# Factors turned by VectorE, a lighter start, and other queues for three pairs' loads, in a state-space and bilinear kernel

## Chip, core and metric

One core of a Trainium2 chip. The metric is the device time of one execution in microseconds, lower is better; the number used is the median over several runs.

## The reference

Two layers, one after the other. The first is a chunked state-space scan over 4 batches, 8 heads, 768 tokens, head width 32, state width 16; the second is a bilinear feed-forward over all 3072 tokens.

```
log_a = log(clip(a, 1e-06, 1))
for each chunk c of 32 tokens:                      # per batch and head
    cum = cumsum(log_a[chunk])
    M = (C B^T) * exp(cum_i - cum_j) * causal
    y[chunk] = M x + (C state) * exp(cum_i)
    state = exp(sum log_a) * state + sum_j B_j x_j exp(cum_last - cum_j)
x2 = y as [3072, 256]                               # token by (head, width)
out = (x2 @ w_a * (x2 @ w_b)) @ w_out               # d_ff = 1536
```

## The kernel before

The kernel uses chunks of 128 tokens instead of 32, six blocks of them, and puts two of the four batches into a *pair*: pair p is block p // 2, batches 2 (p % 2) and the next. There are 12 pairs. Instead of a table of decays it scales B and C. `scan` (VectorE) forms the running products Pr of a in each block; `over_mid` takes the reciprocal rmid of the product at the block's middle. The factors fC = Pr times rmid, by token on partitions, and fB = 1 / fC are made in `factors_mm`: small matmuls of Pr with a selection table selr (which `sel_over_mid` scales by rmid) turn Pr from head-on-partition to token-on-partition. Line 260 is the form for pairs 0 to 3, line 248 that for blocks 2 to 5. The result bank fps is copied to fC by ScalarE (`factors`).

For each pair `scale_bc` multiplies B by fB (bm) and C by fC (cm, or planes for later pairs). The matrices are then turned, by TensorE and copies for pairs 0 to 3 (`transposes`), by a DMA transpose on SP's queue for the others (`turn`, tile `turned`). `scores` multiplies them into the score banks SC, `mask` applies the causal mask (three quarters on VectorE, one on GpSimd behind a ScalarE copy `tmp`), `scale_x` makes x in float16, and `pv` or `outputs` forms y, in X2T or XB, and the state sums. `state_sums` and `state_spread` carry the state from block to block.

The feed-forward runs in units between these steps: `unit` multiplies a pair's y by a slice of Wa and of Wb (tiles aps, bps), ScalarE copies aps to asb (`evac_a`), VectorE multiplies (`times`, hk); `bunit` is the same for a whole block. `out_half` and `bout` multiply hk by Wo and store. All matmul results outside the scores go to four PSUM banks in the order of the string `BANKS`, one digit for each.

The order of the work is written out by hand and kept by each engine. Each engine's own queue also issues its loads: in `load1` one half of a pair (128 KB of x, 64 KB of B or C), in `load2` both halves in one DMA. `loads_bc(p)` issues C and B of pair p, by default from SP's queue, `loads_x(p)` x. Pairs share three input buffers, so a pair's load waits for the readers of the pair three before. SP's queue also carries the turnings and the stores, in order. The weights Wa, Wb, Wo are loaded by GpSimd's queue in two halves each, Wa's first half behind the mask tables (ident at line 201, causal at line 205), which GpSimd fills, and three loads of pair 1 (line 148).

```python
    def loads_bc(p):
        if p < NP:
            tiles(p)
            for w in (1, 0):
                load2(nc.sync, p, w)
```

Of the kernel before, what the change touches and what calls it, by code (L numbers as in the profile page):

```python
# [10 lines left out]
f32 = mybir.dt.float32  # L11
f16 = mybir.dt.float16
# [7 lines left out]
YS = 16.0  # L20

BANKS = (
    "0123102310231012301230123012031230123013201320130213021302130213021320312031203102132013"
    "2013203102310231023103210321032103210321032103210231023102310231023102310231023102310231"
)


# [1 line left out]
def kernel(  # L29
# [66 lines left out]
    planes = [big.tile([128, 6, H * N], f16, name=f"planes{t}") for t in range(2)]  # L96
    causal_q = big.tile([128, Q], f16, name="causal_q")
    Pr = big.tile([BH, NBLK, Q], f32, name="Pr")
    rmid = big.tile([BH, NBLK], f32, name="rmid")
    selr = big.tile([BH, NBLK, 2, NBP * H], f32, name="selr")  # L100
    fB = big.tile([128, NBLK, 2, NBP, H], f32, name="fB")
# [25 lines left out]
    def bank(name):  # L127
        return psf.tile([128, 512], f32, name=name, tag=f"ff{next(banks)}")
# [58 lines left out]
    load1(nc.sync, 1, 0, 0)  # L187
    nc.sync.dma_start(c32, p32_t.ap())
    nc.vector.memset(warm.bitcast(u32), 0)
    nc.vector.memset(zero, 0.0)  # L190
    nc.gpsimd.memset(sel, 1.0)
    nc.gpsimd.affine_select(
# [5 lines left out]
        pattern=[[-H, 2], [-2 * H, NBP], [-1, H]],  # L198
        channel_multiplier=1,
    )  # L200
    nc.gpsimd.memset(ident, 1.0)
    nc.gpsimd.affine_select(
        out=ident, in_=ident, compare_op=ALU.is_equal, fill=0.0, base=0, pattern=[[-1, 128]], channel_multiplier=1
    )
    nc.gpsimd.memset(causal, 1.0)
    for bt in range(2):
        v = causal[64 * bt : 64 * bt + 64]
        nc.gpsimd.affine_select(  # L208
# [16 lines left out]
    def scan(lo, hi):  # L225
        for k in range(lo, hi):
            nc.vector.tensor_tensor_scan(Pr[:, k], a_sb[:, k], zero, 1.0, ALU.mult, ALU.add)
# [12 lines left out]
    def factors_mm(lo, hi, fps=None, k0=0):  # L240
        if fps is None:
            fps = bank("fps")
        w = 2 * NBP * H
        F = fps[:, k0 * w : (k0 + hi - lo) * w].rearrange("p (k r c) -> p k r c", k=hi - lo, r=2)
        for k in range(lo, hi):
            if k * NBP >= P0:
                for c0 in (0, 64):
                    nc.tensor.matmul(
                        F[c0 : c0 + 64, k - lo].rearrange("p r c -> p (r c)"),
                        Pr[:, k, c0 : c0 + 64],  # L250
                        selr[:, k].rearrange("p t c -> p (t c)"),
                        start=True,
                        stop=True,
                        skip_group_check=True,
                        tile_position=(0, c0),
                    )
                continue
            for r in range(2):
                for bt in range(2):
                    nc.tensor.matmul(  # L260
                        F[64 * bt : 64 * bt + 64, k - lo, r],
                        Pr[:, k].rearrange("p (i r) -> p r i", r=2)[:, r],
                        selr[:, k, bt],
                        start=True,
                        stop=True,
                        skip_group_check=True,
                        tile_position=(0, 64 * bt),
                    )
        return F.rearrange("p k r c -> p (k r c)")

    def factors(lo, hi, fps):
        factors_mm(lo, hi, fps)
        nc.scalar.copy(flat(fC, lo, hi), fps[:, 0 : (hi - lo) * 2 * NBP * H])

    def flat(f, lo, hi):
        return f[:, lo:hi].rearrange("p k r b h -> p (k r b h)")

# [4 lines left out]
    def scale_x(p, eng):  # L282
# [5 lines left out]
        else:  # L288
            eng.tensor_scalar(xo, xi, XS, None, ALU.mult)  # L289

    def scale_bc(p, which, eng, factor=None):
        blk, bp = divmod(p, NBP)
        name, f = (("bm", fB), ("cm", fC))[which]
        raw = by_token(pair_in[p][which]) if p >= P0 else pair_in[p][which].rearrange("p h r n -> p r h n")
        if p >= P0 and which:
            eng.tensor_tensor(  # L296
                out=planes[p % 2][:, 4:6].rearrange("p t (h n) -> p t h n", n=N),
                in0=raw,
                in1=f[:, blk, :, bp].unsqueeze(3).broadcast_to((128, 2, H, N)),
                op=ALU.mult,  # L300
            )
            return
        m_ = mid.tile([128, 2, H, N], f16, name=name, tag=name)
        eng.tensor_tensor(  # L304
            out=m_,
            in0=raw,
            in1=(f[:, blk, :, bp] if factor is None else factor).unsqueeze(3).broadcast_to((128, 2, H, N)),
            op=ALU.mult,
        )
        st.setdefault(p, {})[name] = m_  # L310
        if p >= P0:
            dst = planes[p % 2][:, 0:4].rearrange("p (t e) (m f n) -> p t e m f n", e=2, f=2, n=N)
            for e in range(2):
                eng.tensor_copy(dst[:, :, e, :, e], m_.rearrange("p t (m f) n -> p t m f n", f=2)[:, :, :, e])

    def transposes(p, ps=None, between=None, apart=False):
        s = st[p]
        if ps is None:
            ps = [SC[0], SC[1]] if apart else None
            on_dve = apart  # L320
        else:
            on_dve = True
        TB, TC = (TT[:, 0:256], TT[:, 256:512]) if ps is None else [t_.bitcast(f16)[:, 0:256] for t_ in ps]
        for T_, src in ((TB, s["bm"]), (TC, s["cm"])):
            for r in range(2):
                nc.tensor.transpose(
                    T_[:, r * 128 : (r + 1) * 128], src[:, r].rearrange("p h n -> p (h n)"), ident
                )
            if between:
                between()  # L330
                between = None
        BT = mid.tile([128, 2, 2, 2, 64], f16, name="bt", tag="bt")
        CT = mid.tile([128, 2, Q], f16, name="ct", tag="ct")
        b_ = []
        for e in range(2):
            o_ = BT[:, e].rearrange("p r t i -> p (r t i)")
            b_.append(nc.scalar.activation(out=o_, in_=TB, func=AF.Copy, scale=par[:, e : e + 1]))
        c_ = (nc.vector.tensor_copy if on_dve else nc.scalar.copy)(
            CT.rearrange("p t (i r) -> p r (t i)", r=2), TC.rearrange("p (r c) -> p r c", r=2)
        )  # L340
        if apart:
            for i_ in b_:
                tc.declare_no_dep(c_.ins, i_.ins.name, reason="reads of two banks")
        s["BT"], s["CT"] = BT, CT

# [250 lines left out]
    def unit_mm(p, k2, W):  # L596
# [13 lines left out]
                )  # L610
        return ps

    def evac_a(a_ps, on_dve=False):
        asb = ffh.tile([128, 512], f32, name="asb", tag="asb")
        (nc.vector.tensor_copy if on_dve else nc.scalar.copy)(asb, a_ps)  # L615
        return asb
# [90 lines left out]
            eng = nc.gpsimd if (blk, c) == (NBLK - 2, 3) else (nc.sync, nc.scalar)[part]  # L707
            eng.dma_start(rows[:, cs], o_sb[:, 0:w])  # L708

    def loads_bc(p):  # L710
        if p < NP:
            tiles(p)
            for w in (1, 0):
                load2(nc.sync, p, w)

    def loads_x(p, eng=None):
        if p < NP:
            load2(eng or nc.gpsimd, p, 2)

    def fb(k):  # L720
        nc.vector.reciprocal(flat(fB, k, k + 1), flat(fC, k, k + 1))
# [18 lines left out]
    warmup(1, SC[3], 128)  # L740
    scale_bc(0, 0, nc.vector)
    scale_bc(0, 1, nc.vector, v.rearrange("p (r b h) -> p r b h", r=2, b=NBP)[:, :, 0])
    tb, tcp = bank("tb"), bank("tc")
    transposes(0, [tb, tcp], lambda: warmup(1, SC[3], 128))
    nc.scalar.copy(flat(fC, 0, 1), v)
    scan(3, 4)
    warmup(1, SC[3])
    warmup(2, SC[3], 128)
    scores(0)
# [14 lines left out]
    pv_u(0, 1, py, True)  # L764
    for bt in range(2):
        evac0(1, bt, (nc.scalar, nc.vector)[bt], py)
    scan(4, 5)
    w1 = load_w(1)
    for bt in range(2):
        load1(nc.gpsimd, 2, 0, bt)  # L770
    warmup(1, tcp, 128)
    transposes(1, apart=True)
    scan(5, NBLK)
    over_mid(1, NBLK)
    sel_over_mid(1, NBLK, nc.vector)
    aps = [unit_mm(0, 0, Wa), unit_mm(0, 1, Wa)]
    asb = [evac_a(aps[0])]
    nc.gpsimd.tensor_tensor(out=hr, in0=Pr[:, 0:NG, Q - 1], in1=rmid[:, 0:NG], op=ALU.mult)
    nc.gpsimd.tensor_tensor(out=hs, in0=hr, in1=Pr[:, 1:NBLK, 63], op=ALU.mult)
    nc.gpsimd.tensor_tensor(  # L780
# [2 lines left out]
        in1=selb.rearrange("p (b g) -> p b g", b=nb),  # L783
        op=ALU.mult,
    )
    scores(1)
    mask(product(1, 3), by_pool=True)
    aps.append(unit_mm(0, 2, Wa))
    asb.append(evac_a(aps[1]))
    asb.append(evac_a(aps[2]))  # L790
    fps = bank("fps")
    factors(1, NBLK, fps)
    scale_x(1, nc.scalar)
    for m in range(3):
        mask(product(1, m))
    bps = [unit_mm(0, k2, Wb) for k2 in range(3)]
    for bt in range(2):
        load1(nc.gpsimd, 2, 1, bt)
    load_wo(0)
# [9 lines left out]
    for c0 in (0, 64):  # L809
# [7 lines left out]
            tile_position=(0, c0),  # L817
        )
    nc.scalar.copy(G.rearrange("p b g -> p (b g)"), gps[:, 0 : nb * NG])
    for k2 in range(1, 3):  # L820
        times(0, k2, bps[k2], asb[k2])
    fb(1)
# [26 lines left out]
    h = unit(1, 5)  # L849
    scores(2)  # L850
    mask(product(2, 3), by_pool=True)
    mask(product(2, 0))
    mask(product(2, 1))
    mask(product(2, 2))
    h()
    scale_x(2, nc.scalar)
    scale_bc(3, 0, nc.gpsimd)
    scale_bc(3, 1, nc.gpsimd)
    loads_bc(5)
    o = [bank("ops"), bank("ops")]  # L860
    out_mm(0, 0, o[0], range(6))
    out_mm(0, 1, o[1], range(6))
# [59 lines left out]
        return [lambda k=k: bunit(blk, k) for k in ks]  # L922

    scores(3)
    prep(4, (2,))
    mask(product(3, 3), by_pool=True)
    loads_bc(6)
    prep(5)
    loads_x(4, nc.sync)
    loads_x(5, nc.sync)  # L930
# [125 lines left out]
```

## Time and profile before

| | |
|---|---|
| runs | 122.92, 123.72, 124.85; median 123.72 us |
| profiled execution | 122.51 us, span 120.8 us, granted TensorE clock 0.999 |
| busy, share of the span | TensorE 96%, VectorE 71%, ScalarE 60%, GpSimd 52% |
| first unit (line 601) starts | 10.58 us |
| DMA moved | 13.73 MB in 66641 packets, 61616 of them under 512 bytes |
| loads of B or C, 128 KB by SP's queue | median 4.1 (C) and 4.6 us (B) from issue to landing |
| turnings | eight, median 3.2 us from issue to landing |

The span is the time between the first and the last event of the core; the measured time lies 1.7 us above it. An engine's busy share says how much it ran, not that it set the end. In a timeline row the columns are start, duration, engine, line and operation, output and input, and in brackets how long the engine stood idle before it and what released it. `PE` is TensorE, `DVE` VectorE, `ACT` ScalarE, `POOL` GpSimd, `SPq` SP's queue.

### The profile page before, as it was taken

Reading aid. Unit: us, or ns where it says so; the run is one execution under the profiler, and the core shown is the slowest. Engines: PE = TensorE matmul, PEld = TensorE weight load, DVE = VectorE, ACT = ScalarE, POOL = GpSimd, SP = SyncE. Lnnn points to the kernel's source line nnn. Section 1 sums busy time; section 2 is a strip of 40 time slices with the busy share of each in tenths; the row PEclk is TensorE's granted clock in tenths of the full one; section 3 lists DMA queues with packets and bytes.
Section 4 is the critical chain, followed back from the end, with each engine's and each line's share of the span. In section 5 each row is a group of like instructions: output and inputs, shape, how many; then the busy total and the mean of one; then the engine's idle time right before and its main releaser. Section 6 shows DMA issues by size and latency. Waiting matters only on the chain.

```text
span 120.8 us, 3711 instructions
## 1 busy us (share of the span) xinstructions
PE 115.7 (96%) x1455; PEld 79.4 (66%) x1455; DVE 85.2 (71%) x162; ACT 72.1 (60%) x142; POOL 62.3 (52%) x108
## 2 busy tenths in 40 slices
PE   5889999999999999999999999999999999999990
PEld 2445889888898898644476464766464684555890
DVE  1887888882989898499984999677799445847100
ACT  0466757854965767877668637645646737566220
POOL 7999998972795676299731993138400000000200
PEclk9999999999999999999999999999999999999999
DMA  3999999986969999699998874869501012010032
GB/s 62 171 169 233 173 201 159 215 140 70 100 99 126 128 125 144 111 135 146 71 151 111 173 239 126 91 90 159 180 3 49 0 43 87 0 49 0 20 110 87
DMA packets 66641, 13.73 MB, mean 114 GB/s; under 512 B 61616, under 2 KB 66256, under 8 KB 66624
## 3 DMA queue, kind: packets, MB, share of 16 engines
q1 hardware_dynamic: 62448, 9.40, 50.7%
q0 software_dynamic: 2176, 3.74, 17.0%
q10 hardware_dynamic: 2000, 0.36, 1.6%
q8 instruction: 11, 0.18, 0.7%
q14 instruction: 6, 0.05, 0.1%
HBM read 11.13 MB, written 3.15 MB: 118 GB/s over the span
## 4 chain that ended last, share of the span: by engine, by line
PE 89%; DMA 4%; POOL 3%; issue 0%; ACT 0%; POOLq 0%
PE ops L694 18%; PE aps L667 18%; PE bps L667 17%; PE ops L637 9%; PE aps L601 9%; PE bps L601 9%; DMA Wa<-in_moe_w_a_dram 4%; PE SC L358 2%; PE SC L419 2%; POOL cn L148 1%; PE SC L373 1%; PE SC L433 1%; PE SC L508 1%; POOL bn L148 1%; POOL causal L208 1%; PE SC L460 1%
## 5 line engine op out<-in xcount | busy, mean ns | idle before, releaser
L615 ACT COPY asb<-aps 128x512 f32<-128x512 f32 x72 | 41.8, 586 | 14.1 <-PE aps L667 9.7
L679 DVE TENSOR_TENSOR hkb<-bps,asb 128x512 f16<-128x512 f32 x48 | 32.3, 687 | 12.8 <-ACT asb L615 11.6
L667 PE MATMUL aps<-XB,Wa 128*128 128x512 f16 x96 | 28.6, 379 | 0.0
L667 PE MATMUL bps<-XB,Wb 128*128 128x512 f16 x96 | 28.5, 379 | 0.0
L694 PE MATMUL ops<-Wo,hkb 128*128 128x256 f16 (+1 forms) x204 | 22.5, 267 | 0.0
L694 PEld LDWEIGHTS <-hkb 128*128 128x128 f16 x204 | 18.5, 98 | 3.1
L413 DVE TENSOR_TENSOR t<-SC,causal_q 128x512 f16<-128x512 f32 x27 | 17.1, 681 | 3.3 <-PE SC L358 3.3
L622 DVE TENSOR_TENSOR hk<-bps,asb 128x512 f16<-128x512 f32 x24 | 16.2, 685 | 2.4 <-ACT asb L615 1.2
L667 PEld LDWEIGHTS <-Wb 128*128 128x128 f16 x96 | 9.9, 103 | 10.9
L667 PEld LDWEIGHTS <-Wa 128*128 128x128 f16 x96 | 9.7, 103 | 9.1 <-issue 0.2
L708 POOL DMA_DIRECT2D out_dram<-osb x1 | 0.6, 639 | 27.3 <-ACT osb L706 27.3
L706 ACT ACTIVATE osb<-ops 128x256 f32<-128x256 f32 (+1 forms) x16 | 6.0, 376 | 14.3 <-PE ops L694 14.2
L601 PE MATMUL aps<-X2T,Wa 128*128 128x256 f16 x96 | 14.0, 273 | 0.1
L601 PE MATMUL bps<-X2T,Wb 128*128 128x256 f16 x96 | 13.8, 273 | 0.0
L637 PE MATMUL ops<-Wo,hk 128*128 128x256 f16 x96 | 11.5, 273 | 0.0
L601 PEld LDWEIGHTS <-Wa 128*128 128x128 f16 x96 | 9.5, 104 | 1.1 <-DMA Wa<-in_moe_w_a_dram 0.3
L601 PEld LDWEIGHTS <-Wb 128*128 128x128 f16 x96 | 9.8, 103 | 0.6
L411 POOL TENSOR_TENSOR t<-tmp,causal_q 128x512 f16<-128x512 f32 x5 | 5.8, 1159 | 8.0 <-ACT tmp L410 7.9
L637 PEld LDWEIGHTS <-hk 128*128 128x128 f16 x96 | 8.9, 98 | 1.4
L304 POOL TENSOR_TENSOR bm<-bn,fB 128x256 f16<-128x256 f32 x11 | 7.1, 641 | 4.8 <-DMA bn<-in_B_dram 3.6
L289 POOL TENSOR_SCALAR x<-xn 128x512 f16<-128x512 f32 x6 | 8.9, 1489 | 1.0 <-DMA xn<-in_x_dram 0.7
L296 POOL TENSOR_TENSOR planes<-cn,fC 128x256 f16<-128x256 f32 x8 | 5.0, 621 | 7.9 <-DMA cn<-in_C_dram 7.8
(95 smaller groups left out, 124.0 us busy)
## 6 DMA issues: line engine op xcount, KB each, us to landing
out_dram<-osb SPq DMA_DIRECT2D x22, 128.0 KB, 1.8
xn<-in_x_dram SPq DMA_DIRECT2D x7, 256.0 KB, 4.3
cn<-in_C_dram SPq DMA_DIRECT2D x8, 128.0 KB, 4.1
bn<-in_B_dram SPq DMA_DIRECT2D x8, 128.0 KB, 4.6
Wa<-in_moe_w_a_dram POOLq DMA_DIRECT2D x2, 384.0 KB, 5.9
Wb<-in_moe_w_b_dram POOLq DMA_DIRECT2D x2, 384.0 KB, 7.3
Wo<-in_moe_w_out_dram POOLq DMA_DIRECT2D x2, 384.0 KB, 7.2
xn<-in_x_dram POOLq DMA_DIRECT2D x4, 128.0 KB, 7.2
```

What stands on the lines that cost most here:

```text
L289: eng.tensor_scalar(xo, xi, XS, None, ALU.mult)
L304: eng.tensor_tensor(out=m_, in0=raw, in1=(f[:, blk, :, bp] if factor is None else factor).unsqueeze(3).broadcast_to((128, 2, H, N)), op=AL ...
L411: nc.gpsimd.tensor_tensor(out=o_, in0=tmp, in1=c_, op=ALU.mult)
L413: nc.vector.tensor_tensor(out=o_, in0=i_, in1=c_, op=ALU.mult)
L601: nc.tensor.matmul(ps[:, kk * 2 * Q : (kk + 1) * 2 * Q], W[k // 6][:, f, k % 6 // 3 * 384 : (k % 6 // 3 + 1) * 384].rearrange("p (c kk) -> ...
L615: (nc.vector.tensor_copy if on_dve else nc.scalar.copy)(asb, a_ps)
L622: nc.vector.tensor_tensor(out=s["hk"][:, 2 * k2 : 2 * k2 + 2, :].rearrange("p k q -> p (k q)"), in0=b_ps, in1=asb, op=ALU.mult)
L637: nc.tensor.matmul(o_ps[:, 0:d_model], hk[:, k, bt * Q : (bt + 1) * Q], Wo[:, k, :], start=(k == 0), stop=(k == NK - 1), skip_group_check= ...
L667: nc.tensor.matmul(t_, W[k // 6][:, f, k % 6 // 3 * 384 : (k % 6 // 3 + 1) * 384].rearrange("p (c kk) -> p kk c", kk=3)[:, k % 3], XB[:, b ...
L679: return lambda: nc.vector.tensor_tensor(out=s["hk"][:, k], in0=ps[1], in1=asb, op=ALU.mult)
L694: nc.tensor.matmul(o_ps[:, 0:w], hk[:, k, c * Q : (c + 1) * Q], Wo[:, k, cs], start=(k == 0), stop=(k == NK - 1), skip_group_check=True,)
L706: nc.scalar.activation(out=o_sb[:, 0:w], in_=o_ps[:, 0:w], func=AF.Copy, scale=1.0 / (YS * YS))
```

## The change

- The memsets of `ident` and `causal` go from GpSimd to VectorE, after its first memset; GpSimd keeps the selects on them.
- Factors: `factors` and its matmuls now serve block 1 alone, and line 248's form is gone. For blocks 2 to 5 ScalarE multiplies Pr by rmid into a new tile Prm (`over_mid_late`), between the masks of pair 2, and VectorE turns Prm into fC by four 32x32-block transposes (`turn_late`) after a unit's product. `of_pair` reads the other order of these factors.
- Pair 1: both forms of B's turned copy are made by one VectorE product, and C's copy by ScalarE (`joint`); x is scaled half by ScalarE and half by VectorE (`scale_x_split`), after the masks; the scans of blocks 3 and 4 each move up one place; GpSimd does its mask ahead of its three small state products (hr, hs, hsx).
- First units: units 0 and 1 of pair 0 by Wa run with both first halves ahead of both second halves (`units_mm`); the third Wb unit goes behind the state matmuls `gps`.
- Loads: C and B of pair 5 are issued by GpSimd's queue after pair 3's factors; those of pair 6 by SP's queue where pair 5's stood, ahead of the turnings of pairs 4 and 5 instead of between them; x of pairs 10 and 11 in two DMAs each.
- The string BANKS is another one from its 15th digit on.

```diff
+    Prm = big.tile([BH, NBLK, Q], f32, name="Prm")
...
     nc.vector.memset(warm.bitcast(u32), 0)
+    nc.vector.memset(ident, 1.0)
+    nc.vector.memset(causal, 1.0)
     nc.vector.memset(zero, 0.0)
...
-    nc.gpsimd.memset(ident, 1.0)
...
-    nc.gpsimd.memset(causal, 1.0)
...
         for k in range(lo, hi):
-            if k * NBP >= P0:
-                for c0 in (0, 64):
-                    nc.tensor.matmul(
...
-                continue
...
+    def over_mid_late(lo, hi):
+        for k in range(lo, hi):
+            nc.scalar.mul(Prm[:, k], Pr[:, k], rmid[:, k : k + 1])
+
+    def turn_late(lo, hi):
+        for c0 in range(0, Q, BH):
+            nc.vector.transpose(flat(fC, lo, hi)[c0 : c0 + BH].rearrange("p (k c) -> p k c", c=BH), Prm[:, lo:hi, c0 : c0 + BH])
+
+    def of_pair(f, blk, bp):
+        if blk * NBP >= P0:
+            return flat(f, blk, blk + 1).rearrange("p (b r h) -> p b r h", b=NBP, r=2)[:, bp]
+        return f[:, blk, :, bp]
...
+    def scale_x_split(p):
+        X16 = mid.tile([128, H, 2, D], f16, name="x16", tag="x16")
+        xi = pair_in[p][2]
+        st.setdefault(p, {})["X16"] = X16
+        for u in range(2):
+            o_, i_ = [t_[:, 4 * u : 4 * u + 4].rearrange("p h r d -> p (h r d)") for t_ in (X16, xi)]
+            if u:
+                nc.vector.tensor_scalar(o_, i_, XS, None, ALU.mult)
+            else:
+                nc.scalar.mul(o_, i_, XS)
...
+        if joint:
+            b_ = nc.vector.tensor_tensor(
+                out=BT.rearrange("p e r t i -> p e (r t i)"),
+                in0=TB.unsqueeze(1).broadcast_to((128, 2, 256)),
+                in1=par.unsqueeze(2).broadcast_to((128, 2, 256)),
+                op=ALU.mult,
+            )
+            c_ = nc.scalar.copy(
+                CT.rearrange("p t (i r) -> p r (t i)", r=2), TC.rearrange("p (r c) -> p r c", r=2)
+            )
+            tc.declare_no_dep(c_.ins, b_.ins.name, reason="reads of two banks")
...
+    def units_mm(p, ks, W, order):
+        pss = {k2: bank("aps" if W is Wa else "bps") for k2 in ks}
+        for k2, f in order:
+            for kk in range(2):
+                k = 2 * k2 + kk
+                nc.tensor.matmul(
+                    pss[k2][:, kk * 2 * Q : (kk + 1) * 2 * Q],
...
+                    X2T[:, p, :, f],
+                    start=(f == 0 and kk == 0),
+                    stop=(f == 1),
+                    skip_group_check=True,
+                )
+        return [pss[k2] for k2 in ks]
...
-    def loads_bc(p):
+    def loads_bc(p, eng=None):
...
-                load2(nc.sync, p, w)
+                load2(eng or nc.sync, p, w)
...
-            load2(eng or nc.gpsimd, p, 2)
+            if p // NBP == NBLK - 1:
+                for bt in range(2):
+                    load1(nc.sync, p, 2, bt)
+            else:
+                load2(eng or nc.gpsimd, p, 2)
...
+    scan(3, 4)
     tb, tcp = bank("tb"), bank("tc")
...
-    scan(3, 4)
+    scan(4, 5)
...
-    scan(4, 5)
...
-    transposes(1, apart=True)
+    transposes(1, apart=True, joint=True)
     scan(5, NBLK)
     over_mid(1, NBLK)
-    sel_over_mid(1, NBLK, nc.vector)
-    aps = [unit_mm(0, 0, Wa), unit_mm(0, 1, Wa)]
+    sel_over_mid(1, 2, nc.vector)
+    aps = units_mm(0, range(2), Wa, ((0, 0), (1, 0), (0, 1), (1, 1)))
     asb = [evac_a(aps[0])]
+    scores(1)
+    mask(product(1, 3), by_pool=True)
     nc.gpsimd.tensor_tensor(out=hr, ...
...
-    factors(1, NBLK, fps)
-    scale_x(1, nc.scalar)
+    factors(1, 2, fps)
     for m in range(3):
         mask(product(1, m))
-    bps = [unit_mm(0, k2, Wb) for k2 in range(3)]
+    scale_x_split(1)
+    bps = [unit_mm(0, k2, Wb) for k2 in range(2)]
...
     nc.scalar.copy(G.rearrange("p b g -> p (b g)"), gps[:, 0 : nb * NG])
+    bps.append(unit_mm(0, 2, Wb))
...
     mask(product(2, 3), by_pool=True)
+    over_mid_late(2, NBLK)
     mask(product(2, 0))
     mask(product(2, 1))
     mask(product(2, 2))
     h()
+    turn_late(2, NBLK)
     scale_x(2, nc.scalar)
     scale_bc(3, 0, nc.gpsimd)
     scale_bc(3, 1, nc.gpsimd)
-    loads_bc(5)
+    loads_bc(5, nc.gpsimd)
...
     scores(3)
+    loads_bc(6)
     prep(4, (2,))
     mask(product(3, 3), by_pool=True)
-    loads_bc(6)
     prep(5)
```

More of the change, by code (lines that the diff above doesn't have):

```diff
@@ L22 @@
 BANKS = (
-    "0123102310231012301230123012031230123013201320130213021302130213021320312031203102132013"
-    "2013203102310231023103210321032103210321032103210231023102310231023102310231023102310231"
+    "0123102310231032103210321032013210231021302130210321032103210321032130123012301203213021"
+    "3021301203120312031201320132013201320132013201320312031203120312031203120312031203120312"
 )
@@ L245, in factors_mm @@
         for k in range(lo, hi):
-            if k * NBP >= P0:
-                for c0 in (0, 64):
[L248 to L256, printed above, removed]
-                continue
             for r in range(2):
@@ L298, in scale_bc @@
                 in0=raw,
-                in1=f[:, blk, :, bp].unsqueeze(3).broadcast_to((128, 2, H, N)),
+                in1=of_pair(f, blk, bp).unsqueeze(3).broadcast_to((128, 2, H, N)),
                 op=ALU.mult,
@@ L306, in scale_bc @@
             in0=raw,
-            in1=(f[:, blk, :, bp] if factor is None else factor).unsqueeze(3).broadcast_to((128, 2, H, N)),
+            in1=(of_pair(f, blk, bp) if factor is None else factor).unsqueeze(3).broadcast_to((128, 2, H, N)),
             op=ALU.mult,
@@ L314, in scale_bc, with transposes @@
                 eng.tensor_copy(dst[:, :, e, :, e], m_.rearrange("p t (m f) n -> p t m f n", f=2)[:, :, :, e])
-    def transposes(p, ps=None, between=None, apart=False):
+    def transposes(p, ps=None, between=None, apart=False, joint=False):
         s = st[p]
@@ L333, in transposes @@
         CT = mid.tile([128, 2, Q], f16, name="ct", tag="ct")
+        if joint:
[9 more added lines that the diff above has]
+            tc.declare_no_dep(c_.ins, b_.ins.name, reason="reads of two banks")
+            s["BT"], s["CT"] = BT, CT
+            return
         b_ = []
@@ L611, in unit_mm @@
         return ps
+    def units_mm(p, ks, W, order):
[5 more added lines that the diff above has]
+                    pss[k2][:, kk * 2 * Q : (kk + 1) * 2 * Q],
+                    W[k // 6][:, f, k % 6 // 3 * 384 : (k % 6 // 3 + 1) * 384].rearrange("p (c kk) -> p kk c", kk=3)[
+                        :, k % 3
+                    ],
+                    X2T[:, p, :, f],
[4 more added lines that the diff above has]
+        return [pss[k2] for k2 in ks]
     def evac_a(a_ps, on_dve=False):
@@ L785 @@
     )
-    scores(1)
-    mask(product(1, 3), by_pool=True)
     aps.append(unit_mm(0, 2, Wa))
```

## The prediction

> **What bounds the kernel now.** I read the page's totals first, then the chain that ended last, then the timeline around the places that the diff touches. The totals and the slices say that TensorE is the bound at full clock:
>
> ```profile
> PE 115.7 (96%) x1455; PEld 79.4 (66%) x1455; DVE 85.2 (71%) x162; ACT 72.1 (60%) x142; POOL 62.3 (52%) x108
> PE   5889999999999999999999999999999999999990
> PEclk9999999999999999999999999999999999999999
> DMA  3999999986969999699998874869501012010032
> ```
>
> No other engine is above 71%, so an edit matters only where it brings TensorE's first real work forward, takes work off TensorE, or makes TensorE wait. The DMA row is full in the first third; that is where a wait could come from. The chain of waits for the first 16 us (columns: start us, us, what) names the start:
>
> ```profile
> 1.22 0.16 POOL ident L201
> 1.74 0.27 POOL causal L205
> 2.93 0.83 POOL bn L148
> 5.11 5.43 DMA Wa<-in_moe_w_a_dram
> 10.58 1.06 PE aps L601 x8
> ...
> 12.55 0.34 PE fps L260 x8
> 12.90 0.48 PE fps L248 x16
> 13.38 1.43 PE bps L601 x12
> 14.80 0.35 PE SC L433 x32
> ```
>
> GpSimd prepares masks, issues loads, issues Wa at 5.11; Wa lands near 10.5 and the first unit starts at 10.58. From there the chain is almost all matmuls until 118. The sum below is made against the profiled execution: span 120.8, time 122.51; the median of the runs shown is 123.72, 1.21 above it, and I add that at the end.
>
> **The change part by part.** *Masks filled by VectorE.* Two memsets leave GpSimd's head. Their places on the chain: 1.22 to 1.45 and 1.74 to 2.07, so 0.23 + 0.33 = 0.56 us. VectorE fills both after its own 0.27 us memset at 0.92, done by about 1.5; GpSimd's select on ident now waits for that, up to about 0.1; behind it stand the causal selects, three loads and Wa. Wa is thus issued 0.45 earlier. It lands earlier by less, as the 16 engines are 73 to 92% busy between 2 and 5 us and full afterwards: between 0.1 and 0.45. TensorE can't use all of it: the transposes of pair 1 end at 10.45 and wait for GpSimd's bm (9.17 to 9.99), itself behind the mask at 8.05, which started when the x issues ended; that chain gains 0.1. First unit at 10.35 instead of 10.58: gain 0.2 (0.1 to 0.3). The new order of its eight matmuls (both units' first halves first) costs 0: both halves of X2T are there at 10.25.
>
> *Factors of blocks 2 to 5 off TensorE.* L248's 16 matmuls go: 0.48 us off the chain. In their place ScalarE makes four products of 32x128 and VectorE four 32x32-block transposes. No such transpose is in the trace. Rows near by: a 32x128 memset 0.17, a 32x128 scan 0.40; four cost 0.7 to 1.6, and I take 1.0. The four products are bounded by ScalarE's 0.18 (128x32) and 0.38 (128x256) rows: 0.7 to 1.5. Both fall into waits:
>
> ```profile
> 26.21 0.63 ACT L287 ACTIVATE x<-xn 128x512 f16<-128x512 f32 x1 [1.10 <-DMA xn<-in_x_dram]
> 28.59 0.42 DVE L493 TENSOR_SCALAR X2T<-SC 128x256 f16<-128x256 f32 x1 [1.64 <-PE SC L460]
> ```
>
> ScalarE has 1.10 idle before the x of pair 2, and what spills over (0.4 at worst) meets 1.1 of slack to TensorE's use at 28.0. VectorE has 1.64 idle. The new wait is VectorE's, for ScalarE's products, and L493 is queued behind it, which has the 1.64. The factors are ready by about 28.6, and the first reader is the C of pair 4 at 30.14. Cost 0; without the cover it would be the 0.4.
>
> *Pair 1 at the head.* One VectorE product (bounded by 0.68, the 128x512 mask from PSUM, and 0.42, the copy it replaces) takes the place of two ScalarE activations (0.84). It ends near 11.1, scores need it at 11.4: cost 0, and so for the scans, which only change places, and for the smaller selr. GpSimd does its mask before the three small state products: the mask ends 0.8 earlier than its 14.71, the products (0.25 + 0.19 + 0.21) near 14.7, before gps at 15.1. The x of pair 1 is split, half of it on VectorE behind three masks and ahead of the first hk product. With scores at 11.41 to 11.77, masks run 11.95 to 13.85 (1.89 as now), the half x takes 0.35 (between a 0.27 memset and the 0.42 row from PSUM), so pair 1's L433 starts at 14.25 instead of 14.73. TensorE, with only eight bps matmuls ahead of it (the other four moved behind gps), is there at 13.7 and waits 0.55. Then 0.35 + 0.28 + 0.22 for pv, states and gps and 0.44 for the moved unit: next aps at 15.54 against 15.84. So of the possible 0.2 + 0.48 = 0.68 the head keeps **0.30** (0 if x lands no earlier than 13.9 and the halves follow it; 0.68 if masks and x end with TensorE's arrival).
>
> *Loads of pairs 5 and 6.* GpSimd issues C and B of pair 5 right after pair 3's factors, at 27.96. An issue of that kind is in the trace once: 1.23 for 256 KB of 2048 runs. Two cost 1.4 to 2.5, and GpSimd idles 2.18 there and 0.80 later:
>
> ```profile
> 30.14 0.62 POOL L296 TENSOR_TENSOR planes<-cn,fC 128x256 f16<-128x256 f32 x1 [2.18 <-DMA cn<-in_C_dram]
> 31.57 0.62 POOL L304 TENSOR_TENSOR bm<-bn,fB 128x256 f16<-128x256 f32 x1 [0.80 <-DMA bn<-in_B_dram]
> 32.80 1.82 SPq L348 DMA_TRANSPOSE turned<-planes  x1
> 37.28 0.40 PE L358 MATMUL SC<-turned 32*128 32x128 f16 x16
> ```
>
> So the issues themselves are free. Their bytes are not. SP's queue then holds, at the times where pair 5 stood, pair 6's loads, ahead of the turnings of pairs 4 and 5; they wait for pair 3's factors (27.96), over by then. Hardware packets in the DMA view from 28 to 34 us now are 8203, all of pairs 4 and 5 (4 x 2048 runs); the change keeps that number in SP's queue and adds pair 5 through GpSimd's. What that costs: the x that GpSimd loads at 53.41 kept the engines 48% + 59% + 8% of three slices of 1 us = 1.15 us for as many bytes as these two, and the C that SP issued beside it took 6.2 us to land where the median is 4.2. Pair 4's turned planes come later by d, between 0.3 (the idle shares of 32 to 34 us and most of GpSimd's bytes after pair 4's) and 2.0 (that row). I take 1.0, nearer to the 1.15 of engine time. Turned(4) lands at 32.80 + 3.4 = 36.2 and TensorE wants it at 37.28, less the 0.30 won: slack 0.8. **Loss 0.2** (0 to 1.2). Behind that wait stand the score masks of pair 4 and then an ops group; nothing later is out of order. Pair 5's turning gains: it took 4.7 while pair 6's loads ran beside it (others 2.8 to 3.5), and had 0.5 of slack.
>
> By the Trainium skill ("DMA: Bandwidth & Descriptors", section "Queues, rings and completion order") an engine drains a whole packet of one queue row before the next row gets its turn. The page of the profile agrees that the packets differ:
>
> ```profile
> q1 hardware_dynamic: 62448, 9.40, 50.7%
> q0 software_dynamic: 2176, 3.74, 17.0%
> ```
>
> GpSimd's queue moves 1.7 KB a packet, SP's 150 B; by the rule pair 5 would be served ahead of nearly all that SP has queued, d goes to its upper end and the loss to 1.2.
>
> *x of pairs 10 and 11 in halves.* Four SP issues for two: two more at 0.5 to 1.1 each, ending near 81.8 where now they end at 80.7; the turning of pair 11 is issued at 81.79, lands within 3.2, and its scores start at 87.9. Cost 0 by 2.9 us of slack. The other bank numbers still turn over the same four buffers; I cost them at 0, covered by the ScalarE and VectorE evacuations that lead each reuse by a unit (asb ends within 1 us of its unit now).
>
> Sum: -0.30 + 0.2 = -0.1: profiled time 122.4, and on the scale of the median **123.6**.
>
> **The rivals.** *A, all of the head's gain:* masks and x keep up, pair 4 is not late: -0.68, 123.0. For it: the first x half lands at 13.35 already. Against it: VectorE's 1.89 us of masks start only after the scores, and they alone end at 13.85.
>
> *B, slower: pair 4's turned planes stop TensorE.* It decides once d exceeds 0.8. At d = 2.0, the delay of the C beside GpSimd's load, TensorE waits 1.2 before scores(4), -0.30 + 1.2 = +0.9: 124.6. For it: that row, and a DMA share of 0.97 to 1.20 from 29 to 32 us. Against it: GpSimd's bytes flowed some 1.8 us after the issue at 53.41, so from 29.8 here, when pair 4's B is half through. The skill's rule above leads here too.
>
> *C, the delay repeats.* If pair 5 is late by 2 as well (slack 0.5 on its turning), 1.5 comes on top of B's 0.9: +2.4 or somewhat over, about 126.3. Against it: pair 6's loads are gone from beside that turning.
>
> *D, the change does not remove what it says:* products and transposes outgrow their cover and cost 0.4 with a head that gains nothing: 124.1. Against it: 1.10 and 1.64 of idle time.
>
> **How the numbers follow.** Forecast 0.50, A 0.18, B 0.20, C 0.06, D 0.04, something unseen that makes it much faster 0.02. The range for 8 in 10 runs from A to B, with 0.5 on each side for medians that lie between 122.92 and 124.85 in runs of one kernel: 122.4 to 125.0. A measurement tells about 2% from no change, 2.5 us here; only C and a small part of B reach that above, nothing from these rows below. So faster 0.02, within 0.91, slower 0.07.
>
> **What would show it.** Right: no fps matmuls but block 1's eight after the first units; Wa issued near 4.65; first unit near 10.35; a wait of about half a microsecond before pair 1's L433; GpSimd's two issues at 28 to 30.5; a small wait of L358 at pair 4, none at 5 and 6. Wrong: first unit still at 10.58 (then Wa's bytes, not its issue, decide); L433 without a wait (A); L358 of pair 4 waiting over 0.8 us, with SP's turning issued after 34 (B); ScalarE's x of pair 2 ending after 28. A measured time outside 122.4 to 125.0 would mean that a stall or a gain exists that these rows do not show.

## The result, and the profile after

The changed kernel takes 124.24 us in the median (22 runs) against 123.3 (22 runs of the kernel before on the same chip): ratio 1.0078, with a 95% interval of 1.0058 to 1.0097. It is slower by some 0.95 us; 123.6 was forecast. The difference is below 2%, but the interval lies clear of 1. The two medians are of all runs, while the ratios, here and below, compare only the undisturbed ones (15 of the 22 of the changed kernel). Its profiled execution took 123.87, span 122.2, granted clock 1.0, where the kernel before had 122.51 and 120.8.

The totals and slices of the page of the changed kernel:

```profile
PE 117.1 (96%) x1439; PEld 79.4 (65%) x1439; DVE 87.3 (71%) x169; ACT 72.4 (59%) x145; POOL 64.1 (52%) x108
PE   5999999999998999999999999999999999999990
PEclk9999999999999999999999999999999999999999
DMA  3999999999985799999988973898401012010032
```

TensorE has 16 matmuls fewer, as the diff says, and yet 1.4 us more of busy time: its matmuls of the first 10 us ran slower (last section). Apart from the two ends, the one slice of TensorE below 9 is that from 36.7 to 39.7 us. Its cause stands in the chain of waits of the changed kernel, whose pieces there are not TensorE's (columns: start us, us, what):

```profile
19.78 8.06 DMA bn<-in_B_dram
...
27.97 0.50 POOL bm L317
...
28.56 0.62 POOL cm L317
29.18 1.14 POOL cn L158
30.31 0.36 POOL bn L158
...
31.47 0.22 POOL planes L309
...
32.05 0.64 POOL bm L317
...
32.75 0.53 POOL planes L327 x2
...
33.30 5.05 DMA turned<-planes
...
38.40 0.40 PE SC L384 x16
38.80 1.42 PE ops L680 x12
```

Read downwards: pair 3's B lands late, GpSimd scales pair 3, spends its idle time on the two load issues that the change gave it (`cn L158`, `bn L158`), only then scales pair 4, and pair 4's turning takes 5.05 us. In the kernel before, this stretch of the chain is matmuls without a break. The timeline rows of the changed kernel show what TensorE paid, and the head:

```profile
11.37 1.04 PE L644 MATMUL aps<-X2T,Wa 128*128 128x256 f16 x8
14.91 0.48 PE L459 MATMUL SC<-t,x 64*32 64x128 f16 x32 [0.26 <-ACT x L302]
16.29 0.60 PE L627 MATMUL aps<-X2T,Wa 128*128 128x256 f16 x4
38.40 0.40 PE L384 MATMUL SC<-turned 32*128 32x128 f16 x16 [0.56 <-DMA turned<-planes]
```

The first unit is 0.79 later than before, pair 1's pv (L459, L433 before) 0.18 later, the next aps 0.52 later, and pair 4's scores 1.12 later (37.28 before). (L644 is the line of units 0 and 1 in the changed kernel, L627 that of the others, L601 before.) The milestones of TensorE, in us from the start of the span, for these and the other profiles used below:

| profile | first unit | pair 1's pv | next aps | scores 2 | scores 4 | scores 6 | scores 11 | turning of pair 4: issue, us to land |
|---|---|---|---|---|---|---|---|---|
| before | 10.58 | 14.73 | 15.77 | 23.97 | 37.28 | 49.67 | 87.88 | 32.80, 3.4 |
| before again (h1) | 10.75 | 14.95 | 15.95 | 24.15 | 37.47 | 50.20 | 88.41 | 32.91, 3.5 |
| after | 11.37 | 14.91 | 16.29 | 24.46 | 38.40 | 50.79 | 89.23 | 33.30, 5.1 |
| new loads alone (e2) | 10.97 | 15.12 | 16.12 | 24.32 | 38.43 | 51.01 | 89.22 | 33.48, 4.9 |
| pair 5's alone (g2) | 10.76 | 14.90 | 15.90 | 24.10 | 37.41 | 50.42 | 88.63 | 33.35, 2.9 |
| pair 5's alone again (h2) | 10.40 | 14.65 | 15.73 | 23.92 | 38.79 | 51.63 | 89.83 | 34.79, 2.9 |
| pair 6's alone (g3) | 11.09 | 16.51 | 17.51 | 25.70 | 39.36 | 51.75 | 89.96 | 35.91, 3.4 |
| after, old loads (g4) | 11.45 | 15.01 | 16.58 | 24.75 | 38.07 | 50.98 | 89.41 | 33.56, 3.5 |
| same, third unit ahead (f1) | 10.50 | 14.32 | 15.54 | 23.73 | 37.05 | 49.89 | 88.16 | 32.48, 3.3 |
| after, third unit ahead (g1) | 11.44 | 15.40 | 16.40 | 24.60 | 39.26 | 51.65 | 89.93 | 34.06, 5.2 |

A profile is one run; the two of before differ by 0.5 at the end, so only larger steps, or steps that come back in several rows, are read from it.

### The profile page after: what moved, and what is told of

Read it like the earlier page. It is cut to its first block, busy times and chain, and to the rows that moved or that the text cites. A ratio compares the mean times of both kernels' runs of the same rounds, so it can differ in the third digit from the quotient of the medians.

```text
span 122.2 us, 3691 instructions
## 1 busy us (share of the span) xinstructions
PE 117.1 (96%) x1439; PEld 79.4 (65%) x1439; DVE 87.3 (71%) x169; ACT 72.4 (59%) x145; POOL 64.1 (52%) x108
## 4 chain that ended last, share of the span: by engine, by line
PE 78%; DMA 11%; POOL 3%; ACT 3%; issue 2%; DVE 1%; SPq 0%; ACTq 0%; POOLq 0%
PE ops L737 18%; PE bps L710 17%; PE aps L710 17%; DMA bn<-in_B_dram 7%; PE ops L680 5%; DMA turned<-planes 4%; PE SC L221 4%; PE bps L627 3%; PE aps L627 3%; PE tc L221 2%; PE SC L384 2%; PE SC L445 2%; ACT asb L658 1%; POOL bm L317 1%; POOL cn L158 1%
## 5 line engine op out<-in xcount | busy, mean ns | idle before, releaser
L710 PEld LDWEIGHTS <-Wa 128*128 128x128 f16 x96 | 9.7, 103 | 9.1 <-issue 0.2
L627 PE MATMUL bps<-X2T,Wb 128*128 128x256 f16 x96 | 14.0, 273 | 0.0
L627 PE MATMUL aps<-X2T,Wa 128*128 128x256 f16 x88 | 12.9, 273 | 0.0
L627 PEld LDWEIGHTS <-Wb 128*128 128x128 f16 x96 | 9.7, 103 | 0.6
L627 PEld LDWEIGHTS <-Wa 128*128 128x128 f16 x88 | 8.8, 103 | 0.7
L439 DVE TENSOR_TENSOR t<-SC,causal 128x512 f16<-128x512 f32 x12 | 7.6, 680 | 0.7 <-PE SC L399 0.6
```

Source lines behind the costliest of these rows:

```text
L439: nc.vector.tensor_tensor(out=o_, in0=i_, in1=c_, op=ALU.mult)
L627: nc.tensor.matmul(ps[:, kk * 2 * Q : (kk + 1) * 2 * Q], W[k // 6][:, f, k % 6 // 3 * 384 : (k % 6 // 3 + 1) * 384].rearrange("p (c kk) -> ...
L710: nc.tensor.matmul(t_, W[k // 6][:, f, k % 6 // 3 * 384 : (k % 6 // 3 + 1) * 384].rearrange("p (c kk) -> p kk c", kk=3)[:, k % 3], XB[:, b ...
```

## The experiments

Two things could cost time: the head (another order, factors elsewhere) and the new loads. The theories in the expectations are named by letters; "before" and "after" are the two kernels. All were timed against before on the same chip.

**The loads put back, and the loads alone (e1, e2).** e1 is after with

```diff
-    loads_bc(5, nc.gpsimd)
+    loads_bc(5)
...
     scores(3)
-    loads_bc(6)
     prep(4, (2,))
     mask(product(3, 3), by_pool=True)
+    loads_bc(6)
```

and e2 is before with the same edit the other way round.

> The changed kernel with the loads of pairs 5 and 6 where they stood before (both by SP's queue, pair 6 behind pair 4's turning). The changed kernel is 0.78% above the one before. Theory Q (pair 4's turned planes come late because GpSimd's queue and pair 6's loads take the DMA engines): the wait of scores(4) is gone, and the ratio falls from 1.008 to 1.002 or below, about 0.6 us better than the changed kernel. Rival K (the new order of PSUM banks makes TensorE wait for evacuations): ratio stays at 1.006 or above, and the wait near 80 us stays. Rival H (the head does not gain, masks and half x on VectorE hold up pair 1): ratio stays near 1.005.

> The kernel before with the change of loads alone (C and B of pair 5 by GpSimd's queue, those of pair 6 ahead of pair 4's turning). Theory Q: scores(4) wait 0.5 to 0.8 us for the turned planes and the ratio is 1.004 to 1.007. Rivals K and H: ratio 1.000, no wait at pair 4 above 0.2 us.

Measured: e1 1.0109 (1.0079 to 1.0139), e2 1.0067 (1.0045 to 1.0088). So each half of the change alone costs about as much as the whole, 1.0078. The timeline row of pair 4's scores in e2:

```profile
38.43 0.40 PE L358 MATMUL SC<-turned 32*128 32x128 f16 x16 [0.74 <-DMA turned<-planes]
```

Theory Q is right on e2 and wrong on e1, which it put at 1.002 or below. The new loads make TensorE wait 0.74 us at pair 4 with an unchanged head. In e1's profile there is no wait at pair 4; the scores of pair 2 come at 25.66 already, 1.5 us after h1's, so its loss lies in the head. This execution was the slowest of its six, though (125.01), and TensorE's first unit was slow in it (last section); g4 below is the same kernel again.

**Bank order and x of the last pairs put back (e3, e4).** e3 is after with the rest of the old string `BANKS` (two digits swapped for the moved unit), e4 after with

```diff
-            if p // NBP == NBLK - 1:
-                for bt in range(2):
-                    load1(nc.sync, p, 2, bt)
-            else:
-                load2(eng or nc.gpsimd, p, 2)
+            load2(eng or nc.gpsimd, p, 2)
```

> The changed kernel with each matmul result in the bank that it had before (the two digits of gps and the third Wb unit are swapped to follow their new order). Theory K: the wait of a Wb unit for a ScalarE evacuation near 80 us (about 0.3 us) and any such wait at the head are gone, ratio 1.003 to 1.005. Theories Q and H: 1.007 to 1.008, unchanged, unless the old banks fit the new order worse.

> The changed kernel with x of pairs 10 and 11 in one DMA each, as before. Theories Q, K and H: no effect on the end, ratio 1.008 within 0.002. Rival X (the two more DMAs in SP's queue delay pair 11's turning and the stores): 1.006 or less, and the wait near 80 us is gone.

Measured: e3 1.0074 (1.0046 to 1.0101): the bank order costs nothing that shows. e4 1.0133 (1.0102 to 1.0164): the halves of x are not what costs; without them the kernel is rather slower. Why stays open.

**The head taken apart (f1 to f4).** f1 is e1 with the third Wb unit back ahead of pair 1's pv (and its two bank digits swapped back); the edit is shown here. f4 is before with the same edit the other way round, the unit moved behind:

```diff
-    bps = [unit_mm(0, k2, Wb) for k2 in range(2)]
+    bps = [unit_mm(0, k2, Wb) for k2 in range(3)]
...
-    bps.append(unit_mm(0, 2, Wb))
```

f2 is before with the two memsets on VectorE, f3 before with the late factors alone (`over_mid_late`, `turn_late`, `of_pair`, and `factors` for block 1 only).

> The changed kernel with old loads and with the third Wb unit of pair 0 ahead of pair 1's pv again (its bank follows it). Old loads alone stood at 1.011. Theory G (pair 1's x, landed by the DMA engines near 14, sets pv; work moved behind that gate is added to the end, 0.44 us for four matmuls): the unit fills TensorE's wait, ratio 1.005 to 1.008. Rival P (other head edits or the late turnings set the time): ratio stays at 1.010 or above.

> The kernel before with the two memsets moved to VectorE alone. Theory G: Wa is issued 0.37 us earlier, but the engines are full, Wa and x land as before: ratio 1.000 within 0.002. Rival E (an earlier issue lands earlier, as predicted): ratio 0.996 to 0.998. Rival L (GpSimd's early packets push the inputs of pair 0 and x of pair 1 back): 1.002 to 1.005.

> The kernel before with the factors of blocks 2 to 5 made late by ScalarE and VectorE, and nothing else. Theory G: L248's 0.48 us only turns into a longer wait for x ahead of pv of pair 1: ratio 0.999 to 1.001. Rival S (the saved 0.48 is kept): 0.996. Rival V (products and transposes outgrow their cover): 1.002 or above.

> The kernel before with the third Wb unit of pair 0 moved behind gps alone (its bank follows it). Theory G: TensorE waits for pair 1's x and then has 0.44 us of work more behind it: ratio 1.002 to 1.0035. Rival P: ratio 1.000.

Measured: f1 1.0018 (0.9985 to 1.0051), f2 0.9999 (0.9967 to 1.0031), f3 0.9973 (0.9937 to 1.0008), f4 1.0007 (0.9976 to 1.0038). The memsets bring nothing. Theory G is right on f2; f1 and f4 came out below what it said, f3 between G and S. With the third unit ahead of pv the changed head costs nothing that shows; with it behind, some 0.9% (e1) or 0.7% (g4 below). As e1 and f1 differ in nothing but the unit's place and its bank digits, that place is what costs. Yet in the kernel before the same move cost at most 0.38% (f4). f4's interval just takes in the unit's 0.44 us (0.36%), but not e1's whole loss: in the changed head the move costs more than the unit's own work, and the runs do not show all of why.

**Head and loads together, and the two pairs' loads apart (g1 to g4).** g1 is after with f1's edit. g2 is before with `loads_bc(5, nc.gpsimd)` alone; g3 is before with `loads_bc(6)` moved ahead of `prep(4, (2,))` alone; g4 is e1 once more.

> The changed kernel with one edit: the third Wb unit runs ahead of pair 1's pv again, as before the change; all else, the new loads too, as changed. Theory M (the head's loss and the loads' loss lie one behind the other on TensorE's line, and the later one hides the earlier: what the head loses makes TensorE come later to pair 4, whose turned planes land near 38.5 whatever the head does): the next aps unit near 15.6 instead of 16.29, TensorE's wait for turned(4) grows from 0.56 to 1.0 to 1.3, scores(4) at 38.3 to 38.6, and the time stays with that of the new loads alone, 1.0055 to 1.007 of before. Rival N (the loads cost nothing where the head is good, the third unit is the whole loss): no wait over 0.3 at scores(4), 1.000 to 1.003.

> The kernel before with one edit: C and B of pair 5 are issued by GpSimd's queue; those of pair 6 stay where they were, behind the turning of pair 4. Theory P (GpSimd's large packets, served beside SP's small ones, hold up pair 4's B and turning): the turning of pair 4 takes 4.5 us or more to land, TensorE waits 0.5 or more before scores(4), 1.004 to 1.007. Rival O (what counts is how many bytes stand ahead of the turning, by whatever queue; here as many as before): landing 3.0 to 3.7 us, no wait, 0.998 to 1.002.

> The kernel before with one edit: C and B of pair 6 are issued by SP's queue ahead of the turning of pair 4 instead of behind it; pair 5's stay in SP's queue. Theory O (bytes ahead of the turning in SP's queue): pairs 5 and 6 both stand before it, its landing grows from 3.4 to 5 us or more, TensorE waits 0.7 to 1.5 before scores(4), 1.006 to 1.012. Rival P (it is GpSimd's packets that delay): landing below 4 us, no wait over 0.2, 0.998 to 1.002.

> The changed kernel with the loads of pairs 5 and 6 issued as before the change, once more, beside the kernels of this batch. Theory G (in the changed head the third Wb unit stands behind pair 1's x, so its 0.44 us and the idle time ahead of pv are paid; the idle time also lets TensorE's matmuls run at half pace for a while): 1.008 to 1.013 as in the first batch, against 1.002 with the unit ahead. Rival V (that figure was an accident of the first chip's starts): 1.001 to 1.005.

Measured: g1 1.0081 (1.0043 to 1.0118), g2 1.0065 (1.0021 to 1.011), g3 1.0109 (1.0058 to 1.016), g4 1.0085 (1.0044 to 1.0125). g4 repeats e1. In time g1 is near what theory M said: with the new loads the unit's old place, which freed f1 of its loss, is worth nothing. Its row at pair 4:

```profile
39.26 0.40 PE L384 MATMUL SC<-turned 32*128 32x128 f16 x16 [1.12 <-DMA turned<-planes]
```

That is twice the wait of after, as M said. But the way is not M's: the head of this profile was no better than after's. Its first unit waited 0.70 for Wa, the next aps stood at 16.40 (16.29 in after, 15.6 foretold), and pair 4's turned planes landed at 34.06 + 5.2 = 39.2, not near 38.5. What the ratios show is that the two losses do not add up: 1.0109 and 1.0067 alone, 1.0078 together. That a late head shortens the wait at pair 4 fits e2 and after (0.74 and 0.56), but is not shown.

Neither P nor O was right alone, as g2 and g3 both cost. In g3 the turning's landing did not grow (3.4), as O had said; its *issue* came 3 us late, and TensorE waited 0.27 for it. SP's queue in g3's timeline:

```profile
30.80 1.10 SPq L157 DMA_DIRECT2D bn<-in_B_dram  x1
32.00 1.48 SPq L157 DMA_DIRECT2D cn<-in_C_dram  x1
33.53 2.29 SPq L157 DMA_DIRECT2D bn<-in_B_dram  x1
35.91 3.22 SPq L348 DMA_TRANSPOSE turned<-planes  x2
```

The last two loads are pair 6's. The turning stands behind them in program order, and the second needs 2.29 us to be issued. (Its head was late too: pair 1's pv at 16.51, so not all of g3's 39.36 is this.) In g2 the turning landed within 2.9 us and pair 4 did not wait; its profile is that of its fastest run, and the loss could not be seen in it.

**Four more, for what was still open (h1 to h4).** h1 is before unchanged, h2 is g2, h3 is f3, and h4 is f1 with pair 1's x scaled as before:

```diff
     factors(1, 2, fps)
+    scale_x(1, nc.scalar)
     for m in range(3):
         mask(product(1, m))
-    scale_x_split(1)
```

> The kernel before, unchanged, for a second profile of it. Theory N (the first profile, 1.2 us under the median of its runs, had an early head by luck): pair 1's pv at 14.8 to 15.6 instead of 14.73 and the scores of pair 2 at 24.1 to 25.0 instead of 23.97, so that the milestones of the changed head are to be held against these; the scores of pair 4 without a wait. Rival T (23.97 is typical): scores of pair 2 within 0.1 of it. Time 0.997 to 1.003 in both.

> The kernel before with C and B of pair 5 issued by GpSimd's queue, once more. Theory W (the loads' later arrival stops TensorE at one of the next turnings, by an amount that changes from run to run): 1.003 to 1.009, and in a run near the median a wait of 0.4 to 1.2 us for turned planes at pair 4, 5 or 6. Rival Z (its loss was that of disturbed runs): 0.998 to 1.002 and no wait over 0.2.

> The kernel before with the late factors by ScalarE and VectorE alone, once more, and a candidate to beat both kernels. Theory L (the 0.48 us of matmuls leave TensorE's line and nothing takes their place): 0.995 to 0.998. Rival E (what TensorE wins it loses again at the next turned planes, pair 5's or 6's, whose landing does not move): 0.999 to 1.001, with a wait of 0.2 to 0.5 us there.

> The changed kernel with the loads of pairs 5 and 6 and the third Wb unit in their old places, and pair 1's x scaled whole by ScalarE ahead of the masks as before. Theory S (the split x, half of it on VectorE behind three masks, makes pair 1's pv late and eats what the factors win): 0.995 to 0.999. Rival X (the x itself lands that late; who scales it is nothing): 1.000 to 1.004, as with the split.

Measured: h1 0.9999 (0.9972 to 1.0026), h2 1.0019 (0.9979 to 1.0059), h3 1.0014 (0.9984 to 1.0044), h4 1.0037 (1.001 to 1.0064).

h1: pair 1's pv at 14.95 and the scores of pair 2 at 24.15, at the edge of what N said and outside T's. With the head of before, the profiles of the table have 23.92 to 24.32 (25.70 in g3, whose x came late), so the first profile's 23.97 is an early one, by some 0.2. h2: the two intervals of this kernel overlap between 1.0021 and 1.0059, a loss at the edge of what can be told; but this time the profile shows a way in which it comes about, at a place that nobody named. TensorE's and GpSimd's timeline rows in h2:

```profile
28.01 1.19 POOL L157 DMA_DIRECT2D cn<-in_C_dram  x1
29.19 1.15 POOL L157 DMA_DIRECT2D bn<-in_B_dram  x1
33.56 0.62 POOL L304 TENSOR_TENSOR bm<-bn,fB 128x256 f16<-128x256 f32 x1 [2.57 <-PE aps L601]
35.45 1.15 POOL L411 TENSOR_TENSOR t<-tmp,causal 128x512 f16<-128x512 f32 x1
36.65 0.29 PE L433 MATMUL SC<-t,x 64*32 64x128 f16 x12 [1.43 <-POOL t L411]
```

Pair 4's B, issued by SP at 26.58, took 6.8 us to land (3.7 in before, 4.3 in g2) while pair 5's loads of GpSimd's queue ran beside it. GpSimd's product bm for pair 4 waited for that B (the chain of waits has the DMA up to 33.40; the bracket names another releaser), and behind it in program order stands the mask of **pair 3**, for whose pv TensorE stopped 1.43 us. In before bm began at 31.57 and the mask at 33.46. This execution took 124.59, far above what the ratio of 1.0019 says of its kernel: it shows one way to lose time, not the usual run. The wait for turned planes that W had looked for was 0.38, at pair 6, where h1 waits 0.28 with unchanged loads.

h3: with f3, 0.9973 and 1.0014: no gain is shown. Its profile has the reason, in TensorE's row of pair 1's pv:

```profile
13.15 1.49 PE L615 MATMUL bps<-X2T,Wb 128*128 128x256 f16 x12
15.26 0.42 PE L447 MATMUL SC<-t,x 64*32 64x128 f16 x32 [0.61 <-ACT x L301]
```

The sixteen matmuls are gone from TensorE ahead of this row, and TensorE waits 0.61 for pair 1's x, whose landing nothing in the kernel moved (14.49 here, 13.94 in before). Rival E is right on the time, but not on the place: the wait at pair 6 was 0.22, and h1 waits 0.28 there with nothing changed. h4 disproves S: with x whole, as before, h4 is no faster than f1.

No kernel here beats the one before; f3, the nearest, did not repeat its 0.9973.

## Why the prediction was wrong, step by step

The sum was -0.30 for the head and +0.2 for pair 4, -0.1 in all. Measured are +0.95 us for both together. The 124.24 lies inside the stated range, but the way there is another. (The range from A to B with 0.5 on each side is 122.5 to 125.1, not 122.4 to 125.0; and it was drawn around 123.72, the median of three runs of the kernel before, where 22 runs give 123.3.)

*Masks filled by VectorE: 0.2 in hand at the first unit.* Failed. Wa was issued 0.36 earlier (4.75, near the 4.65 foretold), but landed no earlier: the landings, as issue plus duration, run from 10.26 (h2) to 11.05 (g3) in the nine profiles with the old issue, before's 10.54 and h1's 10.70 among them, and from 10.45 (f1) to 11.46 (f2) in the nine with the new one. The prediction's own test, "first unit still at 10.58 (then Wa's bytes, not its issue, decide)", came out that way, or worse; f2's 0.9999 says it is worth nothing in time. The 0.79 by which after's first unit is late is more than Wa: Wa had landed there at 10.76, and TensorE was at its slow first matmuls until 11.37 (last section).

*Head: 0.48 of matmuls off the chain, next aps 0.30 earlier.* Failed in its gate. The prediction let pair 1's pv follow VectorE's masks and the half x behind them, at 14.25, with x landing at 13.35 and 13.9 as in the one profile. In that same profile the copy of x, begun 0.09 behind the landing, ends at 14.66, and pv's weight loads (`PEld`) wait for it:

```profile
14.03 0.63 ACT L287 ACTIVATE x<-xn 128x512 f16<-128x512 f32 x1
14.73 0.24 PEld L433 LDWEIGHTS <-x 64*32 64x32 f16 x32 [0.20 <-ACT x L287]
```

So x was the gate before the change already, and TensorE came to it just in time: with x as late as there, less work ahead of it gains nothing by itself. The second half of x landed between 13.77 (after, f1) and 14.92 (e1) in seventeen of the eighteen profiles, and at 15.74 in g3. In f1, with x at 13.77, pv stood at 14.32, about as foretold; in f4 x landed at 7.27 + 6.82 = 14.09, in e4 at 6.85 + 7.75 = 14.60, and TensorE waited 0.46 and 1.10 for its copy. With x as the gate, what is taken off ahead becomes waiting time (h3), and what is moved from ahead to behind comes on top: with the third Wb unit (0.44) in between, it is 1.38 from pv to the next aps in after, 1.04 in before. In after itself x was there by 13.8, and the gate was ScalarE, which came to it late, behind its copies of the late first units:

```profile
14.41 0.45 ACT L302 ACTIVATE x<-xn 128x256 f16<-128x256 f32 x1
```

The prediction had counted the 0.44 behind pv too, but let a gain in front pay for it. A part of that gain was an error of reading: its 15.84 for the next aps is from the chain of waits, its 14.73 for pv from the timeline, where the next aps starts at 15.77; against that, 15.54 would have been a gain of 0.23.

*Late factors hidden.* Right: ScalarE's products and VectorE's four transposes (1.24 for the four; 1.0 was estimated) cost TensorE no wait in f3 or h3.

*GpSimd's issues free under 2.18 and 0.80 of idle time.* The size was right, the cover was not. The two issues took 1.19 + 1.16 = 2.35, within the 1.4 to 2.5. But the idle time before pair 4's C existed because pair 3's scaling ended at 27.96; in after it ended at 29.18, since pair 3's B landed late. The C of pair 4 was scaled at 31.47 instead of 30.14, and the turning issued at 33.30 instead of 32.80.

*Pair 4's turned planes late by d = 1.0, slack 0.8, loss 0.2.* This term failed by its size. Turned(4) landed at 33.30 + 5.05 = 38.35 against 32.80 + 3.4 = 36.2: d = 2.15, or 1.9 against h1's 36.45. That is the row of 2.0 that the prediction set aside for the 1.15 of engine time. In the profiles of all five kernels with both pairs' loads moved (after, e2, g1; e3 and e4 too) the turning took 4.9 to 5.4 us, in the others of the table 2.9 to 3.5. The slack is spent, and TensorE waits 0.42 (e4) to 1.12 (g1). This is rival B's mechanism, which was put at 0.20. Its +0.9 is almost the measured +0.95, and its 124.6 is above 124.24 only because it was counted from 123.72. But that agreement is luck: B has a wait of 1.2 and a head that gains 0.30, and after has a wait of 0.56 and a head that comes 0.31 late. The rule of the Trainium skill that stood beside the term ("DMA: Bandwidth & Descriptors", section "Queues, rings and completion order") pointed to this upper end. How far packets decide is not settled: with GpSimd's packets alone the turning landed in 2.9 (g2, h2), though pair 4's B once took 6.8, which fits the rule; with both pairs' bytes under way it took 5.

*Rival C, pair 5 late as well:* not seen in after. TensorE ran from scores 4 to scores 5 in 4.37, as before. *D:* the products and transposes stayed within their cover. *x halves and banks at 0:* the banks yes (e3); the halves are no cost.

*How it adds up, against h1.* At the end of the table after is 89.23 - 88.41 = 0.82 behind: scores 2 +0.31; scores 4 another +0.62, which is the 0.56 wait; scores 6 gives back 0.34, since pair 6's turned planes, for which h1 waits 0.28, are there when the later TensorE comes; the rest, +0.23, arises before scores 10, where ScalarE's XB waits 0.47 for VectorE's U. It is no accident of one run: from scores 9 to scores 10 TensorE takes 9.48 or 9.49 in after, e1, e3, e4 and g4, 9.33 or 9.34 in f1 and g1 (where that wait is 0.32), and 9.27 or 9.28, without it, in before, h1, e2, g2, h2, g3, f2, f4 and h3. In h4, which differs from f1 only in that pair 1's x is scaled whole, it is 9.27 too; so the split of x is under suspicion, by one profile, and why it should tell at 78 us stays open. Neither the banks (e3) nor the x halves at the end (e4) are its cause.

What stays open besides: e1 and g4 lose 1.05 us or more, of which up to 0.44 may be the third unit, 0.2 is this wait, and in g4 0.46 a wait for turned(5); that the last one comes from the head rather than by chance is not shown.

## What to carry to other kernels

Before a move is credited with the time that it takes off an engine, ask what the next instruction waits for: ahead of a gate set by a transfer, less work is only more waiting, and work put behind the gate comes on top. Idle time on an engine that issues loads is cover only in the profile that shows it; where the idle time is itself a wait for a transfer, price it with that transfer late. And a queue that works in order passes a delay to whatever stands next in its program, here from pair 4's load to pair 3's mask.

## What the runs showed that was not expected

The first matmuls of nearly the same code run at one of two paces. A warm-up matmul of 128x512 in the timeline of before takes 0.38 us from about 4.6 us on:

```profile
7.96 0.38 PE L220 MATMUL tc<-warm 128*128 128x512 f16 x1
```

Of the eighteen profiles sixteen have come to this pace by 7.4 us. In the timeline of after, and in f2's, most of them still take 0.6 until about 10 us, although the pages of before and after give 9 (90% or more) for the granted clock in every slice:

```profile
9.42 0.62 PE L221 MATMUL tc<-warm 128*128 128x512 f16 x1
```

A row of five of them takes 1.25 in before; f2's profile, with the slow start too, needs 2.23 and still ran 123.53, in the middle of its runs. Nor is the slow start what the change costs: e3 and e4, with the changed loads and head and the fast pace, reach the scores of pair 11 at 89.64 and 89.29, after at 89.23. e1 was fast by then, but fell back to the slow pace after a wait of 0.88 us for Wa:

```profile
11.42 1.84 PE L644 MATMUL aps<-X2T,Wa 128*128 128x256 f16 x8 [0.88 <-DMA Wa<-in_moe_w_a_dram]
```

The same eight take 1.04 in after, and 1.05 in g1 behind a wait of 0.70. By the Trainium skill ("TensorE: Matmul & The Clock Gate", "Part 1: The HAM clock gate (the "warmup" mystery)") TensorE runs at half clock until a window of about 3.4 us has been busy, and the moment of the change moves by half a microsecond from run to run. The traces agree on two paces, but the moment differs by some 5 us between these profiles.
